# Talking-heads attention and a feed-forward layer on one core: second head mixing on 64x64 tiles, a new ordering pass, one ring of accumulator banks

## Chip, cores and metric

One core of one Trainium2 chip runs the whole program. The metric is the device time of one execution in microseconds (us); the kernel before takes 929.02 us as the median of three runs (928.87 to 931.21). Engines are called as in the profile: PE (matrix multiply) with its weight loads PEld, DVE (vector), ACT (scalar), POOL (GpSimd) and SP (which issues the DMAs).

## What is computed

Four batches, 12 heads, 448 positions, 64 elements per head, model width 768, feed-forward width 2048:

```python
scores = scale * np.matmul(q, k.transpose(0, 1, 3, 2))
scores = np.einsum('bhij,hg->bgij', scores, w_pre)      # first mixing of the heads
attn = softmax(scores, axis=-1)
attn = np.einsum('bhij,hg->bgij', attn, w_post)         # second mixing
x = np.matmul(attn, v)                                  # heads side by side: 1792 x 768
h = x @ w_in
out = (h * sigmoid(1.702 * h)) @ w_out
```

The feed-forward weights arrive as 64-bit floats, everything else as 32-bit floats.

## The kernel before

**Attention.** The unit of work is a step: 10 query rows of one batch, so 45 steps per batch and 180 in all. Score products (`scores`, tile `qk`) are made for blocks of about 112 rows, written to DRAM (`sd`) and read back (`gather`, tile `r`, four buffers) with one partition per row and head. `mix_two` (L321) mixes the heads of two steps in four 64x64 products (tile `mx`), `peak` takes row maxima on DVE, `expo` the exponential and row sums on ACT (tile `e`), `shifted`, `inverse` and `weigh_mix` divide the mixing matrix by the sums (tile `wr`). `post` (L368) is the second mixing. It turns the attention around at the same time, so that positions j come to lie on partitions: the exponentials are the stationary operand in four slices of CP = 112 columns, for two halves of the rows (a = 0, 1), and `wr` is the moving operand with 60 columns. That is 8 products of 32-bit floats for one step, into one pair of accumulator banks (tile `pp`, one buffer):

```python
for jc in range(NR):
    for a in range(2):
        rs = slice(a * GAP, a * GAP + w)
        nc.tensor.matmul(pp[:CP, a, jc*w:(jc+1)*w], e[rs, jc*CP:(jc+1)*CP], wr[rs, :, :n], ...)
```

The pair is then copied out by ACT (`keep_whole`, first two batches) or split into two 16-bit parts by ACT and DVE (`keep_upper`, `keep_lower`). `context` (tile `av`) multiplies by V.

**Feed-forward.** 32 units (8 slices of the width for each of 4 batches). A unit has 36 products in `hidden` (L578, tile `h`) and 36 in `project` (L622, tile `po`), in 16-bit floats with two parts per operand. The weights of a slice are converted once (`conversion`, L484: ACT, POOL and DVE make two 16-bit parts in the tile `w_p`, tag `wc`, one buffer), stored to DRAM (`wd`, `store`) and loaded again for each of the four batches (`fetch_w`, L574, tile `wt`: 64 loads of 768 KB).

**What sets the order.** Nothing is ordered by the hardware or a library: `add` (L676) notes each job with its engine, an assumed duration, a due time and the buffers that it takes; `run_all` (L740) goes through the jobs once, always taking one that can start soonest and is due first, and writes the instructions in that order. Where it foresees an idle stretch of PE it has `fill` (L287) put in products of a matrix of ones whose result is not used (L290). Accumulator banks come from a pool: six single banks in turn (`gen`) and the one pair (`pp`).

Of the kernel before, what the change touches and what calls it, by code (L numbers as in the profile page):

```python
# [1 line left out]

# [34 lines left out]
NR, CP = 4, S // 4  # L37
NCC = DM // 128
NS = 8
# [6 lines left out]
def attention_then_feed_forward(ctx, tc, q, k, v, w_pre, w_post, w_in, w_out, out):  # L46
# [16 lines left out]
    NBK = 6  # L63
# [54 lines left out]
    def add_over(parts):  # L118

        p, n = parts.shape  # L120
        t = bank(f"sums_{len(first_sum)}")[:, :n]
        first_sum.append(n)
        nc.tensor.matmul(t, ones[:p, :], parts, start=True, stop=True)
        return t
# [6 lines left out]
    SH = {"q": [128, NPAIR // THIRDS, S], "k": [128, NPAIR // THIRDS, S], "v": [CP, H // THIRDS, NR * D]}  # L131
# [55 lines left out]
    def pair_of(name, b, i):  # L187

        key = (name + "p", b, i)
        if key not in st:  # L190
            if name == "v":
                st[key] = flow.tile([CP, 2, H // THIRDS, NR * D], F16, name=f"vp{i}_{b}", tag=f"vp{i}")
# [33 lines left out]
    def bank(name, tag="gen", bufs=NBK):  # L226
        return ps.tile([128, 512], F32, name=name, tag=tag, bufs=bufs)

    def scores(b, c, pr, tag=("gen", NBK)):

        i0, n = block(b, c)
        two = [bank(f"qk_{b}_{c}_{pr}_{x}", *tag) for x in range(2)]
# [82 lines left out]
    def mix(i):  # L315
        mx = row["mx", i] = bank(f"mx_{i}")
        fill(mx)
        r = row.pop(("r", i))
        nc.tensor.matmul(mx[:, :S], wa, r[:KG], start=True, stop=True)  # L319

    def mix_two(two):  # L321

        tiles = []
        for y, i in enumerate(two):
            mx = row["mx", i] = bank(f"mx_{i}")
# [42 lines left out]
    def post(i):  # L368
# [26 lines left out]
    def keep_whole(i):  # L395
        nc.scalar.copy(mixed_to(i), row.pop(("pp", i)))  # L396
# [10 lines left out]
    def context(b, c, pr):  # L407
        i0, n = chunk(b, c)
        if pr % 3 == 0:
            av = bank(f"av_{b}_{c}_{pr}")  # L410
# [4 lines left out]
        if not AV16[b]:  # L415
            for jc in range(NR):
                for d in range(2):
# [3 lines left out]
                        st["v", b, h // w][:, h % w, jc * D:(jc + 1) * D],  # L421
# [5 lines left out]
        for t, (jc, i, j) in enumerate(terms):  # L427
            for d in range(2):
# [3 lines left out]
                    st["vp", b, h // w][:, i, h % w, jc * D:(jc + 1) * D],  # L432
# [47 lines left out]
    NP = 3  # L480
    HW = WN // NP
    WF = 5

    def conversion(kind, s):  # L484

        nm = f"w{kind}_{s}"
        src = (w_in, w_out)[kind][s]
# [83 lines left out]
    wt = {}  # L571
# [6 lines left out]
    def hidden(u, fc, part):  # L578

        s, b = units[u]  # L580
        if part == 0:
            st["h", u, fc] = bank(f"h_{u}_{fc}")[:, :S]
            fill(st["h", u, fc])
# [38 lines left out]
    def project(u, e):  # L622
        g, w = gt[u], wt[1, u].rearrange("p t (f e) -> p t f e", e=DM)
        po = st["po", u, e] = bank(f"po_{u}_{e}")[:, :S]
# [37 lines left out]
    COUNT = {"r": NRB, "e": 3, "wr": NWR, "pp": 1, "gen": NBK, "sc": 3, "p": 2, "x": 2,  # L662
# [4 lines left out]
    waiting, lanes = [], []  # L667
# [6 lines left out]
    MODE = {"qk": 1, "pp": 1, "mx": 2, "av": 3}  # L674

    def add(eng, occ, f, after=(), due=0.0, lat=None, size=0.0, takes=(), kind="", bias=0.0, behind=None, moves=""):  # L676

        occ = occ if isinstance(occ, dict) else {e: occ for e in eng.split("/")}
        if lat is None:
# [3 lines left out]
             "kind": kind, "moves": moves, "bias": bias, "left": 0, "then": [], "next": [], "at": None, "from": 0.0}  # L683
# [9 lines left out]
        if not j["left"]:  # L693
            waiting.append(j)
# [10 lines left out]
    def room_for(j, e):  # L705

        at, need = 0.0, {}
        for x in j["takes"]:
            if len(x) == 2 or x[2] == e:
# [8 lines left out]

    def take(j, e):
        for x in j["takes"]:  # L720
            if len(x) == 2 or x[2] == e:
                have = held[x[0]]
                if len(have) >= COUNT[x[0]]:
                    done = [(over_when(h), n) for n, h in enumerate(have) if over_when(h) is not None]
                    have.pop(min(done)[1])
# [14 lines left out]
    def run_all():  # L740

        last = ""
        while waiting:
            picks = []
            for e in list(free) + ["-"]:
# [15 lines left out]
                if best:  # L761
                    t = min(x[0] for x in best) + LOOK
                    picks.append(min((x for x in best if x[0] <= t), key=lambda x: (x[2]["due"] - (2.0 if e == "PE" and last in MODE and x[2]["kind"] in MODE else 0.0), x[0]))[1:] + (e,))
            assert picks, [(j["eng"], j["due"], [x[0] for x in j["takes"]]) for j in waiting][:20]
            s, j, e = min(picks, key=lambda x: (x[0], x[1]["due"]))
            waiting.remove(j)
# [18 lines left out]
            log.append((s, e, j))  # L785
            j["by"] = e
            settle(j, at, e, 0.0 if j["size"] else CROSS)
            j["f"](e) if len(j["eng"]) > 1 else j["f"]()
            gap[0] = 0.0

    log = []
# [44 lines left out]
    idle = ps.tile([128, 512], F32, name="idle", tag="gen", bufs=NBK)  # L836
# [67 lines left out]
    tags = [("gen", NBK)]*3  # L904
    near = st["near"] = mixed.tile([CI, H, S], F32, name="near", tag="p")
    for pr in range(NPAIR):
        two = scores(0, 0, pr, tags[pr % 3])
# [14 lines left out]
    held["gen"] = [12.0, 12.2, 12.6, 12.9, 13.2, 13.5]  # L922
# [18 lines left out]
    def step_tasks(i):  # L941
# [4 lines left out]
        if i < GPC:  # L946
# [3 lines left out]
            if i < AHEAD:  # L950
                m["from"] = READY[i]
        else:
            if g % 2 == 0:
                two = [i, i + 1] if g + 1 < GPB else [i]
                for x in two:
                    mx_home[x] = []
                m = add("PE", 0.77, lambda: mix_two(two), [gathers[x] for x in two] + [mixes.get(i - 1), mixers.get(b)], i - 1,
                        takes=[("gen", mx_home[x]) for x in two], kind="mx")
# [14 lines left out]
        p = add("PE", 0.44, lambda: post(i), [w, e, posts.get(i - 1)], i + 1, takes=[("pp", pp)], kind="pp")  # L973
# [104 lines left out]
    def conversion_tasks(kind, s, first):  # L1078
# [17 lines left out]
        for a in range(NP):  # L1096
            u = add("A", 0.62, lambda a=a: c["w_upper"](a, "A"), [k] + low[:0] + ([ups[0]] if a else []), due + 0.5, 0.72,
                    takes=[] if a else [("wc", pair)])
# [6 lines left out]
        pair.append(j)  # L1105


    at_scores = {}
# [65 lines left out]
    for u in range(NU + 1):  # L1174
        for fc in range(2):
# [4 lines left out]
            if u:  # L1180
                quanta += [("p", u - 1, e) for e in range(3 * fc, 3 * fc + 3)]
    due_of = {q: BEGIN + n / RATE for n, q in enumerate(quanta)}
    g_done, rests = {}, {}
    wt_home = {(kind, u): [] for kind in range(2) for u in range(NU)}
    got = {}
    for u in range(NU):
        s, b = units[u]
        due = due_of["h", u, 0, 0]
        for kind in range(2):
            got[kind, u] = add("SP", 0.4, lambda kind=kind, u=u: fetch_w(kind, u),  # L1190
                               [conv_done[kind, s]] + gated_by(min(int(due) - 14, N)), due - 6 + 3 * kind,
                               size=0.786, takes=[(f"wt{kind}", wt_home[kind, u])], kind="late", behind=got.get((kind, u - 1)), moves="wt")
        g_home, lower_g = [], []
        for fc in range(SF):
            gen, th = [], []
            j = None
            for x in range(3):
                due = due_of["h", u, fc, x] - 1.5 * (x > 0)
                j = add("PE", 1.134, lambda u=u, fc=fc, x=x: hidden(u, fc, x), [got[0, u], x_done[b], j], due,
                        takes=[] if x else [("gen", gen)], kind="ff")  # L1200
# [15 lines left out]
        for e in range(NCC):  # L1216
            due = due_of["p", u, e]
            gen, pt = [], []
            j = add("PE", 1.134, lambda u=u, e=e: project(u, e), [got[1, u], *lower_g], due, takes=[("gen", gen)], kind="ff")
            g_home.append(j)  # L1220
            wt_home[1, u].append(j)
# [5 lines left out]
            def both(by, u=u, e=e, s=s, b=b, k=(k := {})):  # L1227
                collect(u, e, by)
                if by == "D" or s == 0:
                    k["rest"]["eng"], k["rest"]["occ"], k["rest"]["lat"] = ("-",), {"-": 0.0}, {"-": 0.0}  # L1230
# [3 lines left out]
                     {x: rest[x] + 0.1 for x in eng.split("/")}, takes=takes, bias=0.8)  # L1234

# [16 lines left out]
def _layout(inputs):  # L1252
# [4 lines left out]
    a["v"] = a["v"].reshape(B, H, NR, CP, D).transpose(0, 3, 1, 2, 4).reshape(B, CP, H, NR * D)  # L1257
# [26 lines left out]
```

## Time and profile before

| | us |
|---|---|
| median of three runs | 929.02 |
| profiled execution, its own time | 927.6 |
| span of its instructions | 925.9 |
| PE busy | 901.5 |
| ACT busy | 562.6 |
| DVE busy | 542.5 |

A timeline row gives the start, the time from the first start to the last end, the engine, the line of the kernel, the operation, the tile written and those read, sizes and count. Products are pipelined, so that a row reaches into the next one: what a group costs is the distance from its start to the start of the next group. A product of 32-bit floats is two weight loads and two matmul records.

### The profile page before, as it was taken

The page shows a single profiled execution, that of the slowest core. Times are in us where ns is not written, and L with a number is a line of the kernel's source. Part 1 is how long each engine was busy: PE and PEld are TensorE (multiplying, and loading weights), DVE is VectorE, ACT ScalarE, POOL GpSimd, SP SyncE. Part 2 cuts the span into 40 slices and gives each one's busy share as a digit, 9 for nine tenths or more (in the row PEclk, how much of TensorE's full clock was granted, in tenths as well). Part 3 has the DMA queues.
Part 4 walks back from the last instruction along what each step waited for, and adds up shares of the span by engine and source line. Part 5 has one row for each costly group of instructions (what it writes and reads, how often), then busy time and mean ns, then how long its engine had stood idle before and what let it go on. Part 6 is the DMA issues. An engine that isn't in the chain of part 4 may idle for free.

```text
span 925.9 us, 22628 instructions
## 1 busy us (share of the span) xinstructions
PE 901.5 (97%) x8708; PEld 548.3 (59%) x8708; DVE 542.5 (59%) x1254; ACT 562.6 (61%) x1280; POOL 264.6 (29%) x518
## 2 busy tenths in 40 slices
PE   8998998999999999989999999999999999999998
PEld 4676676556565665655656555555656555555554
DVE  4656665876768977975456755457544553333233
ACT  4867776887678697854576565555555453323442
POOL 1312332332223513351116322332123332203332
PEclk9999999999999999999999999999999999999999
DMA  6878888889878998776677585466544322344322
GB/s 218 279 234 264 268 292 267 301 297 286 301 250 284 293 319 273 254 242 212 208 249 225 159 263 164 142 206 214 174 142 125 126 95 69 123 142 137 137 70 93
DMA packets 68270, 194.42 MB, mean 210 GB/s; under 512 B 10419, under 2 KB 35123, under 8 KB 68163
## 3 DMA queue, kind: packets, MB, share of 16 engines
q1 hardware_dynamic: 68163, 192.98, 63.9%
q8 instruction: 69, 1.13, 0.5%
q14 instruction: 38, 0.31, 0.1%
HBM read 136.32 MB, written 54.04 MB: 206 GB/s over the span
## 4 chain that ended last, share of the span: by engine, by line
PE 89%; DVE 5%; ACT 2%; DMA 2%; issue 1%; POOL 0%; SPq 0%; ACTq 0%; DVEq 0%; POOLq 0%
PE h L589 23%; PE po L628 23%; PE pp L377 16%; PE mx L333 7%; PE av L419 4%; PE qk L239 3%; PE av L430 3%; PE pp L290 3%; PE qk L249 3%; PE mx L319 1%; DMA qf<-in_q_dram 1%; ACT p L396 1%; DVE w_f L518 1%; DVE nm L338 1%; DVE w_p L557 1%
## 5 line engine op out<-in xcount | busy, mean ns | idle before, releaser
L589 PE MATMUL h<-x,wt 128*128 128x448 f16 x1152 | 244.2, 353 | 0.0
L628 PE MATMUL po<-g,wt 128*128 128x448 f16 x1152 | 241.4, 353 | 0.1
L377 PEld LDWEIGHTS pp<-wr,e 60*112 60x112 f32 (+1 forms) x2880 | 158.3, 175 | 62.9 <-issue 40.0
L377 PE MATMUL pp<-wr,e 60*112 60x60 f32 (+1 forms) x2880 | 177.8, 262 | 0.0
L628 PEld LDWEIGHTS <-wt 128*128 128x128 f16 x1152 | 108.9, 98 | 113.6 <-issue 17.9
L589 PEld LDWEIGHTS <-wt 128*128 128x128 f16 x1152 | 108.4, 98 | 103.5 <-issue 6.6
L656 POOL TENSOR_TENSOR acc<-acc,pt 128x448 f32<-128x448 f32 x83 | 99.6, 1201 | 149.6 <-ACT pt L650 141.4
L355 POOL TENSOR_SCALAR rs<-sm 124x1 f32<-124x1 f32 x180 | 44.5, 247 | 328.0 <-ACT e L345 325.4
L345 ACT ACTIVATE e<-mx,nm 124x448 f32<-124x448 f32 x180 | 114.6, 637 | 20.9 <-DVE nm L338 20.0
L338 DVE TENSOR_REDUCE nm<-mx 124x1 f32<-124x448 f32 x180 | 107.7, 616 | 26.8 <-PE mx L333 20.0
L608 DVE SCALAR_TENSOR_TENSOR th<-th,h 128x448 f32<-128x448 f32 x64 | 39.6, 619 | 137.1 <-ACT th L604 136.9
L650 ACT ACTIVATE pt<-po,ct 128x448 f32<-128x448 f32 x83 | 52.4, 633 | 84.4 <-PE po L628 81.6
L404 DVE TENSOR_TENSOR p<-pp,p 112x480 f16<-112x480 f32 (+1 forms) x90 | 58.7, 652 | 70.9 <-ACT p L400 70.8
L400 ACT CAST p<-pp 112x480 f16<-112x480 f32 (+1 forms) x90 | 50.5, 562 | 72.0 <-PE pp L377 71.5
L333 PE MATMUL mx<-r,wq 60*64 60x448 f32 (+1 forms) x672 | 84.5, 562 | 0.0
L396 ACT COPY p<-pp 112x480 f32<-112x480 f32 (+1 forms) x90 | 51.1, 567 | 40.1 <-PE pp L377 39.3
L604 ACT ACTIVATE th<-h,ct 128x448 f32<-128x448 f32 x64 | 40.5, 633 | 55.5 <-PE h L589 55.2
L652 DVE SCALAR_TENSOR_TENSOR acc<-po,ct,acc 128x448 f32<-128x448 f32 x85 | 57.6, 680 | 23.4 <-PE po L628 23.2
L260 ACT COPY sc<-qk 112x448 f32<-112x448 f32 (+1 forms) x124 | 61.8, 539 | 13.9 <-PE qk L249 9.2
L614 ACT ACTIVATE g<-th,gs 128x448 f16<-128x448 f32 x64 | 42.8, 668 | 24.3 <-DVE th L608 23.8
L508 POOL TENSOR_SCALAR w_f<-w_f 128x512 f32<-128x512 f32 x48 | 32.1, 670 | 74.3 <-ACT w_f L504 73.3
L366 POOL TENSOR_SCALAR wr<-wp,rs 124x60 f32<-124x60 f32 (+1 forms) x90 | 38.9, 433 | 48.6 <-DVE rs L360 34.7
(137 smaller groups left out, 1018.3 us busy)
## 6 DMA issues: line engine op xcount, KB each, us to landing
wt<-wd SPq DMA_DIRECT2D x64, 768.0 KB
r<-sd SPq DMA_DIRECT2D x317, 105.0 KB
sd<-sc SPq DMA_DIRECT2D x84, 392.0 KB
w<-in_moe_w_in_dram SPq DMA_DIRECT2D x24, 512.0 KB
w<-in_moe_w_out_dram SPq DMA_DIRECT2D x24, 512.0 KB
wd<-w_p SPq DMA_DIRECT2D x16, 768.0 KB
out_dram<-acc SPq DMA_DIRECT2D x24, 224.0 KB
kf<-in_k_dram SPq DMA_DIRECT2D x6, 448.0 KB
```

Of the source, the lines that this page charges most:

```text
L260: (nc.scalar.copy if eng == "A" else nc.vector.tensor_copy)(t[:n, x, :], two[x][:n, :S])
L333: nc.tensor.matmul(out, w[rs], r[rs], start=True, stop=True)
L338: nc.vector.tensor_reduce(nm[:K], row["mx", i][:K, :S], axis=AX.X, op=ALU.max, negate=True)
L345: nc.scalar.activation(e[:K], row.pop(("mx", i))[:K, :S], AF.Exp, bias=row.pop(("nm", i))[:K, 0:1], accum_out=sm[:K, 0:1],)
L377: nc.tensor.matmul(pp[:CP, a, jc * w:(jc + 1) * w], e[rs, jc * CP:(jc + 1) * CP], wr[rs, :, :n], start=True, stop=True,)
L396: nc.scalar.copy(mixed_to(i), row.pop(("pp", i)))
L404: nc.vector.tensor_tensor(p[1], row.pop(("pp", i)), p[0], op=ALU.subtract)
L589: nc.tensor.matmul(h, w[:, i, c, fc * 128:(fc + 1) * 128], x[:, j, c, :], start=(n == 0), stop=(n == len(terms) - 1),)
L628: nc.tensor.matmul(po, w[:, j, fc, e * 128:(e + 1) * 128], g[:, i, fc, :], start=(n == 0), stop=(n == len(terms) - 1),)
L650: nc.scalar.activation(pt, po, AF.Copy, scale=c)
L652: nc.vector.scalar_tensor_tensor(a, po, c, a, op0=ALU.mult, op1=ALU.add)
L656: nc.gpsimd.tensor_tensor(a, a, st.pop(("pt", u, e)), op=ALU.add)
```

## The change

1. `post` works on 64x64 tiles: each slice of 112 positions is cut in two of CJ = 56, which go to the lower and the upper 64 partitions. The lower one loads 64 columns (8 of them over again, against zero rows that `_layout` puts into V). A step has 16 products in the place of 8. The kept tiles have CP = 120 partitions, V tiles 128.
2. The eight banks form one tile, `banks`. The ordering pass gives out bank numbers; a step takes any two neighbours.
3. `run_all` goes through the jobs up to 15 times without writing: after each forward pass, `latest` goes backward from the end and finds how late each job could start; these times rank the jobs in the next pass. The best pass is written. The assumed duration of `post` is the same as before.
4. Converted weights are written straight into the `wt` buffers that the first batch reads (`DIRECT = 0`), besides the store to DRAM; the first batch's 16 loads fall away.
5. Loads of the 64-bit weights may start 20 steps earlier, `mix_two` is queued behind an earlier `post`, and `keep_whole` may run on ACT or DVE.

Cut to its core:

```diff
-NR, CP = 4, S // 4
+NR, CJ = 4, S // 8
+CP = 64 + CJ
...
-        pp = ps.tile([128, 2, 512], F32, name=f"pp_{i}", tag="pp", bufs=1)
+        pp = bank(2)
         fill(pp[:, 0])
         for jc in range(NR):
-            for a in range(2):
-                rs = slice(a * GAP, a * GAP + w)
-                nc.tensor.matmul(
-                    pp[:CP, a, jc * w:(jc + 1) * w], e[rs, jc * CP:(jc + 1) * CP], wr[rs, :, :n],
-                    start=True, stop=True,
-                )
+            for d in range(2):
+                j0, m = (2 * jc + d) * CJ, CJ if d else GAP
+                for a in range(2):
+                    rs = slice(a * GAP, a * GAP + w)
+                    nc.tensor.matmul(
+                        pp[d * GAP:d * GAP + m, a, jc * w:(jc + 1) * w], e[rs, j0:j0 + m], wr[rs, :, :n],
+                        start=True, stop=True,
+                    )
...
+        to = dict(tag=f"wt{kind}", bufs=2) if s >= DIRECT else dict(tag="wc", bufs=1)
...
-                t["p"] = flow.tile([128, 2, WN], F16, name=f"{nm}_p", tag="wc", bufs=1)
+                t["p"] = flow.tile([128, 2, WN], F16, name=f"{nm}_p", **to)
+                if s >= DIRECT:
+                    wt[kind, s] = t["p"]
...
-    MODE = {"qk": 1, "pp": 1, "mx": 2, "av": 3}
+    MODE = {"qk": 1, "pp": 2, "mx": 2, "av": 3}
...
+        for n in range(PASSES + 1):
+            reset(ranks)
+            order = one_pass(False)
+            if order is None:
+                break
+            end = max(j["at"] for j in jobs)
+            if best is None or end < best[0]:
+                best = end, ranks, STAY[0]
+            ENDS.append(end)
+            ranks = latest(order)
+            STAY[0] = STAYS
+        reset(best[1])
+        STAY[0] = best[2]
+        one_pass(True)
...
-            q = add("A", 0.47, lambda: keep_whole(i), [p], i + 2, 0.58, takes=takes_p)
+            q = add("A/D", {"A": 0.47, "D": 0.53}, lambda e: keep_whole(i, e), [p], i + 2, {"A": 0.58, "D": 0.62}, takes=takes_p, bias=0.3)
...
-            j = add("SP", 0.4, lambda a=a: c["fetch"](a), gated_by(first + 2 * a), first + 2 * a, size=0.524, takes=[("w64", w64)], kind="late", moves="w64")
+            j = add("SP", 0.4, lambda a=a: c["fetch"](a), gated_by(first + 2 * a - 20), first + 2 * a, size=0.524, takes=[("w64", w64)], kind="late", moves="w64")
```

How the order moves, counted over the whole program: products of ones fall from 176 to 94; the places where PE goes from one tile shape (128x128, 64x128, 128x64, 64x64) to another fall from 463 to 346; the copies of L396 that go to DVE are 17 of 90; `collect` goes to ACT and POOL 70 times in the place of 83, to DVE 98 in the place of 85; loads `wt<-wd` fall from 64 to 48. The first feed-forward product stands behind the 47th `post` before, behind the 45th now.

PE, before, around the end of the first chunk of 12 steps (`r`: gathered scores, `p`: kept attention, `vf`: V):

```order
L333 MATMUL mx_750<-r_663,wq 64x448 x2
L333 MATMUL mx_751<-r_668,wq 64x448 x2
L419 MATMUL av_0_3_770<-p_0_311,vf_0_547 64x120 x8
L419 MATMUL av_0_3_770<-p_0_311,vf_0_632 64x120 x16
L377 MATMUL pp_834<-wr_824,e_767 112x60 x8
L290 MATMUL pp_864<-ones 128x128 x4
L377 MATMUL pp_864<-wr_831,e_808 112x60 x8
```

and the same place now:

```order
L345 MATMUL banks<-r_628,wq 64x448 x2
L345 MATMUL banks<-r_660,wq 64x448 x2
L391 MATMUL banks<-wr_774,e_762 64x60 x2
L391 MATMUL banks<-wr_774,e_762 56x60 x2
L391 MATMUL banks<-wr_774,e_762 64x60 x2
L391 MATMUL banks<-wr_774,e_762 56x60 x2
L391 MATMUL banks<-wr_774,e_762 64x60 x2
L391 MATMUL banks<-wr_774,e_762 56x60 x2
L391 MATMUL banks<-wr_774,e_762 64x60 x2
L391 MATMUL banks<-wr_774,e_762 56x60 x2
```

A second mixing of eight products over 112 positions is now sixteen over 64 and 56; it stands right behind a first mixing, with the same tile shape, and the context product that stood between them has moved.

SP, before, where the first batch's weights are loaded for the first time (`w`: 64-bit weights, `sd`: scores):

```order
L497 DMA w_2_64_0_2023<-in_moe_w_out_dram 128x1024
L264 DMA sd_0_97<-sc_0_4_2011 112x896
L576 DMA wt_0_2064<-wd_0_109 128x3072
L264 DMA sd_0_97<-sc_0_5_2057 112x896
L264 DMA sd_1_98<-sc_1_2_2075 112x896
```

and now:

```order
L583 DMA wd_0_118<-w_0_p 128x3072
L515 DMA w_2_64_0_2223<-in_moe_w_out_dram 128x1024
L276 DMA sd_1_98<-sc_1_2_2189 112x896
L276 DMA sd_1_98<-sc_1_3_2200 112x896
L276 DMA sd_0_97<-sc_0_4_2226 112x896
L515 DMA w_2_64_1_2307<-in_moe_w_out_dram 128x1024
```

The store of converted weights remains, later than before; the load of them for the first batch is gone.

## Rows read from the trace of the kernel before

**Rows 1.** The page: span, then busy time of each engine, share, instructions.

```profile
span 925.9 us, 22628 instructions
PE 901.5 (97%) x8708; PEld 548.3 (59%) x8708; DVE 542.5 (59%) x1254; ACT 562.6 (61%) x1280; POOL 264.6 (29%) x518
```

**Rows 2.** The page: the chain that ended last, by engine and by line.

```profile
PE 89%; DVE 5%; ACT 2%; DMA 2%; issue 1%; POOL 0%; SPq 0%; ACTq 0%; DVEq 0%; POOLq 0%
PE h L589 23%; PE po L628 23%; PE pp L377 16%; PE mx L333 7%; PE av L419 4%; PE qk L239 3%; PE av L430 3%; PE pp L290 3%; PE qk L249 3%; PE mx L319 1%; DMA qf<-in_q_dram 1%; ACT p L396 1%; DVE w_f L518 1%; DVE nm L338 1%; DVE w_p L557 1%
```

**Rows 3.** Busy time by stretch, all engines: length, PE, PEld, DVE, ACT, POOL, clock, DMA share, GB/s.

```profile
0.00:20.00 20.00, 17.31 (x72) 9.69 (x72) 8.82 (x25) 8.68 (x18) 1.80 (x15) 1.00 0.60 208
20.00:160.00 140.00, 131.25 (x1506) 95.57 (x1506) 84.95 (x215) 102.19 (x252) 40.74 (x105) 0.99 0.85 271
160.00:420.00 260.00, 251.25 (x2447) 156.19 (x2444) 204.46 (x489) 196.23 (x469) 87.42 (x166) 0.99 0.85 280
420.00:785.00 365.00, 364.61 (x3842) 214.91 (x3841) 199.71 (x434) 206.03 (x464) 96.21 (x198) 1.00 0.55 174
785.00:926.00 141.00, 137.12 (x853) 71.99 (x851) 44.55 (x91) 49.51 (x81) 38.46 (x34) 1.00 0.33 115
```

**Rows 4.** The same stretches, products of ones (L290) alone: PE, PEld.

```profile
20.00:160.00 140.00, 29.40 (x198) 24.94 (x198) 0.99 0.85 271
160.00:420.00 260.00, 21.71 (x148) 19.29 (x148) 0.99 0.85 280
420.00:785.00 365.00, 1.20 (x6) 0.82 (x6) 1.00 0.55 174
```

**Rows 5.** Timeline of PE, 511.9 to 516.4 us.

```profile
510.78 1.30 PE L628 MATMUL po<-g,wt 128*128 128x448 f16 x6
511.92 1.30 PE L589 MATMUL h<-x,wt 128*128 128x448 f16 x6
513.15 1.00 PE L377 MATMUL pp<-wr,e 60*112 60x60 f32 x16
514.07 0.98 PE L333 MATMUL mx<-r,wq 60*64 60x448 f32 x8
514.99 1.31 PE L628 MATMUL po<-g,wt 128*128 128x448 f16 x6
```

**Rows 6.** Timeline of PE, 66 to 69 us: a post between products of its own tile shape.

```profile
66.97 0.91 PE L377 MATMUL pp<-wr,e 60*112 60x60 f32 x16
67.71 0.96 PE L239 MATMUL qk<-kf,qf 64*104 64x448 f32 x4
```

**Rows 7.** Timeline of PEld in 5 ns windows at 513.32 and 513.42 us.

```profile
513.24 0.18 PEld L377 LDWEIGHTS pp<-wr,e 60*112 60x112 f32 x2
...
513.34 0.18 PEld L377 LDWEIGHTS pp<-wr,e 60*112 60x112 f32 x2
```

**Rows 8.** Timeline of PEld at 514.07 and 514.23 us, and of PE at 514.48 us.

```profile
514.07 0.15 PEld L333 LDWEIGHTS mx<-r,wq 60*64 60x64 f32 x4
...
514.13 0.15 PEld L333 LDWEIGHTS mx<-r,wq 60*64 60x64 f32 x4
...
514.07 0.61 PE L333 MATMUL mx<-r,wq 60*64 60x448 f32 x4
```

**Rows 9.** Timeline of PE, two context products and what follows each.

```profile
503.18 2.08 PE L430 MATMUL av<-p,vp 112*64 112x120 f16 x72
505.20 1.12 PE L628 MATMUL po<-g,wt 128*128 128x448 f16 x5
...
593.89 1.60 PE L430 MATMUL av<-p,vp 112*64 112x88 f16 x72
595.42 0.80 PE L377 MATMUL pp<-wr,e 60*112 60x60 f32 x12
```

**Rows 10.** Groups by form on PE: busy us, mean ns, idle before, what ended it.

```profile
L290 PE MATMUL pp<-ones 128*128 128x128 f32 x204 | 28.8, 292 | 12.9 <-ACT p L396 9.4 <-DVE p L404 2.1 <-DVE rs L360 1.5
```

**Rows 11.** Second mixing (L377) alone in the third and fourth stretch: PE, PEld.

```profile
160.00:420.00 260.00, 55.10 (x896) 49.10 (x896) 0.99 0.85 280
420.00:785.00 365.00, 78.18 (x1264) 68.84 (x1264) 1.00 0.55 174
```

**Rows 12.** The page, groups of POOL, DVE and ACT that move (columns as in rows 10).

```profile
L656 POOL TENSOR_TENSOR acc<-acc,pt 128x448 f32<-128x448 f32 x83 | 99.6, 1201 | 149.6 <-ACT pt L650 141.4
...
L650 ACT ACTIVATE pt<-po,ct 128x448 f32<-128x448 f32 x83 | 52.4, 633 | 84.4 <-PE po L628 81.6
L404 DVE TENSOR_TENSOR p<-pp,p 112x480 f16<-112x480 f32 (+1 forms) x90 | 58.7, 652 | 70.9 <-ACT p L400 70.8
...
L396 ACT COPY p<-pp 112x480 f32<-112x480 f32 (+1 forms) x90 | 51.1, 567 | 40.1 <-PE pp L377 39.3
...
L652 DVE SCALAR_TENSOR_TENSOR acc<-po,ct,acc 128x448 f32<-128x448 f32 x85 | 57.6, 680 | 23.4 <-PE po L628 23.2
```

More of the change, by code (lines that the diff above doesn't have):

```diff
@@ L315, in mix @@
     def mix(i):
-        mx = row["mx", i] = bank(f"mx_{i}")
+        mx = row["mx", i] = bank()
         fill(mx)
@@ L707, in room_for @@
         at, need = 0.0, {}
+        at = min((x[0] for x in places(j)), default=None) if any(x[0] in BANKS for x in j["takes"]) else 0.0
+        if at is None:
+            return None
         for x in j["takes"]:
+            if x[0] in BANKS:
+                continue
             if len(x) == 2 or x[2] == e:
@@ L762, in run_all @@
                     t = min(x[0] for x in best) + LOOK
[L763 to L766, printed above, removed]
+                    picks.append(min((x for x in best if x[0] <= t), key=lambda x: (x[2]["rank"] - (STAY[0] if e == "PE" and last in MODE and x[2]["kind"] in MODE else 0.0), x[0]))[1:] + (e,))
+            if not picks:
+                return None
+            s, j, e = min(picks, key=lambda x: (x[0], x[1]["rank"]))
+            del waiting[next(n for n, x in enumerate(waiting) if x is j)]
             take(j, e)
@@ new lines, in latest, with last_place, put @@
+    def latest(order):
+        end = max(j["at"] for j in jobs)
+        over = {}
+        used = {e: ([], []) for e in [*free, "ring", "port"]}
+        def last_place(use, ub, width):
+            starts, ends = use
+            x = bisect.bisect_left(starts, ub + width) - 1
+            t = ub
+            while x >= 0 and ends[x] > t:
+                t = min(t, starts[x] - width)
+                x -= 1
+            return t
+        def put(use, s, t):
+            starts, ends = use
+            x = bisect.bisect_left(starts, s)
+            if x < len(starts) and starts[x] <= t + 1e-9:
+                t = max(t, ends[x])
+                del starts[x], ends[x]
+            if x and ends[x - 1] >= s - 1e-9:
+                ends[x - 1] = max(t, ends[x - 1])
+            else:
+                starts.insert(x, s)
+                ends.insert(x, t)
+        left = {id(j): len(j["then"]) + len(j["next"]) + len(j["frees"]) for j in jobs}
+        before = {id(j): [] for j in jobs}
+        for j in jobs:
+            for x in j["then"] + j["next"] + j["frees"]:
+                before[id(x)].append(j)
+        ready = [(-j["at"], n) for n, j in enumerate(jobs) if not left[id(j)]]
+        number = {id(j): n for n, j in enumerate(jobs)}
+        heapq.heapify(ready)
+        while ready:
+            j = jobs[heapq.heappop(ready)[1]]
+            e = j["by"]
+            gap = 0.0 if j["size"] else CROSS
+            by = [end]
+            for x in j["then"]:
+                by.append(over[id(x)] - (0.0 if e == "-" else SAME if x["by"] == e else gap))
+            by += [over[id(x)] - CROSS for x in j["frees"]]
+            by = min(by)
+            if j["size"]:
+                width = j["size"] / 16 / DMA["rate"]
+                t = last_place(used["ring"], by - DMA["late"] - MARGIN.get(j["moves"], 0.0) - width, width)
+                put(used["ring"], t, t + width)
+                t -= DMA["issue"]
+            else:
+                t = by - j["lat"][e]
+            t = min([t] + [over[id(x)] - 0.01 for x in j["next"]])
+            if e != "-":
+                width = j["occ"][e]
+                uses = [used[e]] + [used["port"]] * (j["kind"] == "two" and e in "DG")
+                old = None
+                while old != t:
+                    old = t
+                    for u in uses:
+                        t = last_place(u, t, width)
+                for u in uses:
+                    put(u, t, t + width)
+            over[id(j)] = t
+            for x in before[id(j)]:
+                left[id(x)] -= 1
+                if not left[id(x)]:
+                    heapq.heappush(ready, (-x["at"], number[id(x)]))
+        assert len(over) == len(jobs)
+        low = min(over.values())
+        return [over[id(j)] - low for j in jobs]
@@ L957, in step_tasks @@
                 m = add("PE", 0.77, lambda: mix_two(two), [gathers[x] for x in two] + [mixes.get(i - 1), mixers.get(b)], i - 1,
-                        takes=[("gen", mx_home[x]) for x in two], kind="mx")
+                        takes=[("gen", mx_home[x]) for x in two], kind="mx", behind=posts.get(i - 3))
                 for x in two:
@@ L972, in step_tasks @@
         w = add("G", 0.35, lambda: weigh_mix(i), [v], i, 0.3, takes=[("wr", wr)])
-        p = add("PE", 0.44, lambda: post(i), [w, e, posts.get(i - 1)], i + 1, takes=[("pp", pp)], kind="pp")
+        p = add("PE", 0.44, lambda: post(i), [w, e, posts.get(i - 1)], i + 1, takes=[("two", pp)], kind="pp")
         wr.append(p)
@@ L1105, in conversion_tasks @@
         pair.append(j)
+        if s >= DIRECT:
+            wt_home[kind, s] = pair
+            got[kind, s] = low
+            wt_taken[kind, s] = ups[0]
+    wt_home = {(kind, u): [] for kind in range(2) for u in range(B * NS)}
+    got, wt_taken = {}, {}
     at_scores = {}
```

159 lines of the change are left out of this document (115 added, 44 removed).

## Prediction, made blind

> **What bounds the kernel now.** I read the page first: PE is busy 97% of the span, ACT 61%, DVE 59% [rows 1], and the chain that ended last lies on PE for 89% [rows 2]. A busy PE alone proves little, since products overlap and some are made only to fill. So next the stretches. From 420 us on PE is never idle: 364.6 of 365 us busy, while DVE and ACT work 200 and 206 us [rows 3]; whatever PE is spared there comes off the end, as long as the other engines keep up. Before that PE is idle for 8.75 us in 20-160 and 8.75 us in 160-420 (length less busy time), and 29.4 and 21.7 us more go to products of ones [rows 3, 4]. Idle time and fillers together are 17.9 + 52.3 = 70 us in which PE stood and something else was late. The last 141 us are feed-forward alone, and the granted clock is 0.99 to 1.00 throughout, so it is no term. So nearly all of the time is PE's own work, and the question is what that work costs when it is cut differently.
>
> The costly item is the second mixing, 16% of the chain [rows 2]. The timeline shows one post starting at 513.15 and its successor at 514.07: 0.92 us [rows 5]. Of this a part is the change of tile shape: six feed-forward products take 1.14 us when their own kind follows and 1.23 us when a post follows [rows 5], so a change costs 0.09 us. A post between products of its own shape takes 0.74 us [rows 6]. Inside it the weight loads set the pace: two of 112 columns, one for each half of the rows, start every 0.10 us [rows 7], eight times (16 records). Its 60 moving columns hide under that.
>
> **The change part by part.**
>
> *Second mixing.* Now a post has 16 products, 32 pairs of weight load and matmul record, spread over four tiles: eight rounds of four. The first mixing already shows such a round: four loads of 64 columns start together at 514.07, the next four at 514.13, and four matmuls run side by side [rows 8]. That is 0.06 us for a round. By columns it would be 0.74 / 8 x 64 / 112 = 0.053 us. I take 0.057, between them, as the row's two decimals leave that open: 8 x 0.057 = 0.46 us. The saving is 0.28 us for each of 180 posts: 51 us (47 at 0.06, 57 at 0.053). On the path are all 180 as far as PE is the last to be ready: 45 of them lie before 160 us, 56 in the second stretch, 79 after 420 (x896 and x1264, 16 to a post) [rows 11].
>
> Here the skill speaks against the change. The Trainium skill, page "TensorEngine Tiling (Array Packing)", section Instruction Overhead, puts about 60 cycles on each matmul and advises against taking a tiling factor from a dimension that is already small; 60 moving columns are small. By that, as an estimate from the page, 32 pairs at 25 ns are 0.80 us, and the second mixing would gain nothing. The trace so far contradicts it where several tiles are in use: 72 pairs in 593.89 to 595.42 are 21 ns each, over two tiles only [rows 9], and the four matmuls above need no such spacing [rows 8]. What no row shows is 32 pairs in a row over four tiles; this is the first rival and the third.
>
> *Changes of shape.* The order has 117 fewer (463 to 346), since first and second mixing now share a shape and the order groups them: 117 x 0.09 = 10.5 us, all on PE. Where PE waits anyway it is worth nothing; most of the places lie in the stretch without waits, so I keep it.
>
> *Waits and fillers (70 us now).* The single pair of `pp` banks made PE wait 9.4 us for ACT's copy and 2.1 us for DVE's before fillers [rows 10]; with any two of eight banks these 11.5 us can go. The order has 82 fewer products of ones; at 52.3 us for 176 they cost 0.30 us each, so 24 us, if nothing else is late in their place. Against it: PE arrives earlier at each wait, by about 0.3 us in a step, so that part of the wait that is now hidden behind a slow post comes out. Bounds: nothing is gained (PE waits 70 us as before), or only the 94 products are left (28 us, a gain of 42). I take 20, the bank waits and a third of the fillers, and not more, because 160-420 has DVE at 79% and DMA at 85% [rows 3].
>
> *Weights written in place.* 16 loads of 768 KB go: 12.6 MB, about 45 us of the DMA's rate of 280 GB/s, in a stretch where DMA is 85% busy [rows 3]. No wait of PE on these loads is in the chain [rows 2], so the sum takes nothing for it; it is the room that lets the other transfers keep up. The price is a new wait: from the third unit on, ACT's first `w_upper` needs the buffer of the unit two before it, and in ACT's queue exponentials stand behind it, on which PE's posts depend. Between lies a unit of 72 products, 72 x 0.19 = 13.7 us by [rows 5] (1.14 us for six), so I price it at nothing; without that cover each of twelve such places could cost the microseconds of one conversion.
>
> *Moved work.* 17 copies go from ACT to DVE (0.65 us each by the nearest DVE row, 0.57 on ACT), 13 collections from ACT and POOL to DVE (0.68 us; 0.63 and 1.20 saved) [rows 12]: DVE gets 20 us more, ACT 18 less, POOL 16 less. Hidden after 420 us (DVE 55% busy); in 160-420 it uses up part of the room. V tiles grow by a seventh and the copies from 112 to 120 partitions with the same 480 elements: nothing.
>
> **Sum.** Against the profiled execution: 927.6 - 51 - 10.5 - 20 = 846. The median of the runs shown is 1.4 us above that execution (929.0), so I predict **847 us**. With the ends of the three terms this likeliest case runs from 929 - 57 - 10.5 - 42 = 819 to 929 - 47 - 10.5 - 0 = 872.
>
> **Rivals.**
>
> *1. The pairs do not follow each other that fast.* If 32 pairs need the 21 ns of the context run [rows 9], a post takes 0.68 us, the saving is 0.06 x 180 = 11 us in the place of 51, and the time is 887. For it: nothing in the trace is denser over so many pairs. Against: that run is itself filled by its moving columns (88 over two tiles), so 21 ns is an upper bound, and rows 8. Chance 0.10.
>
> *2. The early stages are held by something else.* If DVE, DMA and the step's own chain (mixing, maximum, exponential, sum, product) keep 20-420 at its length, only 79 posts and their share of the changes count: 22 + 5 = 27 us, time 902. For it: DMA 85% busy, DVE 204 of 260 us [rows 3]. Against: PE's own work, fillers left out, is still 73% and 88% of the two stretches, ACT and DVE in 20-160 are at 73% and 61%, and a sixth of the DMA bytes of the second stretch leave. Chance 0.11.
>
> *3. Slower: the pairs run one after another whatever their tile.* The place is L391. At the 28 ns of the 120-column context run (2.02 us for 72 [rows 9]) a post takes 32 x 0.028 = 0.90 us, 0.16 more, 28 us in all; less 10.5 for the changes of shape and with the waits as they are, 947. It decides from 25 ns on: there a post takes 0.80 us and the changes of shape are just used up. For it: twice as many instructions through one queue. Against: rows 8. Chance 0.03 for this, and 0.03 for ending within the bound of no change, around that point. By the skill's page above it would be this point exactly.
>
> **How the numbers follow.** 0.73 for the forecast, 0.10 and 0.11 for the first two rivals, 0.03 and 0.03 for the rest. A measurement of this kernel tells about 0.3%, 3 us, from no change. Faster: 0.73 + 0.10 + 0.11 = 0.94; same 0.03; slower 0.03. The range is 818 to 885: the likeliest case with its ends, and most of the first rival; the second stays out.
>
> **What would show it.** Right: eight rounds of four weight loads in a post, one every 0.053 to 0.06 us; a post between feed-forward products taking about 0.65 us in the place of 0.92; PE above 97% after some 380 us, the all-feed-forward end as long as before (about 140 us); `pp` waits on copies gone. Wrong: rounds of 0.085 us or more (rival 1), PE idle or filling for 100 us or more in the first half (rival 2), a post over 0.9 us (rival 3).

## The result and the profile after

The changed kernel takes 851.61 us (median of four runs, 850.99 to 851.93) against 928.94 us for the kernel before in the same comparison: a ratio of 0.9163, 95% interval 0.9146 to 0.9181. The prediction was 847, range 818 to 885. The profiled execution has a span of 849.2 us where the one before had 925.9. The ratios here and below take executions in the fast state only; of the four in the first set with the old second mixing that leaves two, 899.76 and 912.78 us.

The page of the changed kernel: busy time, share and instructions of each engine, then the chain that ended last, by engine and by line.

```profile
PE 817.7 (96%) x11424; PEld 475.8 (56%) x11424; DVE 561.7 (66%) x1281; ACT 548.5 (65%) x1255; POOL 259.1 (31%) x503
...
PE 75%; DVE 8%; ACT 7%; DMA 6%; issue 3%; POOL 1%; SPq 0%; ACTq 0%; DVEq 0%; POOLq 0%
PE banks L608 23%; PE banks L647 22%; PE banks L391 9%; PE banks L345 6%; PE banks L251 3%; PE banks L444 3%; PE banks L433 3%; PE banks L261 2%; PE banks L302 2%; DMA r<-sd 2%; ACT e L357 1%; ACT waste L114 1%; DMA sd<-sc 1%; ACT sc L272 1%; DVE w_p L577 1%
```

PE works 84 us less, with more instructions. The second mixing (now L391) has gone from 16% of the chain to 9% [rows 2], and the chain leaves PE more often: 25% of it lies elsewhere, 11% before.

The stretches of the changed kernel, cut so that each holds as many posts as in [rows 3]: 45, 56 and 79. The other work in them is not quite the same: 24 feed-forward products already lie in the first one. All engines:

```profile
20.00:145.00 125.00, 112.73 (x2212) 77.95 (x2209) 92.21 (x238) 96.92 (x246) 45.27 (x107) 0.99 0.89 295
145.00:378.00 233.00, 223.78 (x3202) 127.34 (x3200) 202.94 (x472) 193.21 (x459) 91.97 (x161) 0.98 0.81 266
378.00:708.00 330.00, 326.24 (x5073) 187.29 (x5072) 211.30 (x455) 198.00 (x449) 81.73 (x187) 0.99 0.60 194
708.00:850.00 142.00, 137.49 (x856) 72.30 (x854) 44.62 (x91) 49.75 (x81) 38.55 (x35) 1.00 0.33 114
```

The second mixing alone, PE and PEld (x1440, x1792 and x2528 are 45, 56 and 79 posts of 32 records, as many as before):

```profile
20.00:145.00 125.00, 29.96 (x1440) 25.43 (x1440) 0.99 0.89 295
145.00:378.00 233.00, 38.67 (x1792) 31.83 (x1792) 0.98 0.81 266
378.00:708.00 330.00, 53.80 (x2528) 47.05 (x2528) 0.99 0.60 194
```

The products of ones alone:

```profile
20.00:145.00 125.00, 19.77 (x124) 16.79 (x124) 0.99 0.89 295
145.00:378.00 233.00, 9.53 (x64) 8.66 (x64) 0.98 0.81 266
378.00:708.00 330.00, 0.00 (x0) 0.00 (x0) 0.99 0.60 194
```

The three stretches were 140, 260 and 365 us [rows 3]; now they are 125, 233 and 330: 15, 27 and 35 us shorter. The feed-forward end is as long as before. Fillers have gone from 52.3 to 29.3 us [rows 4], but PE's idle time in the three stretches has risen from 17.9 to 25.2 us (length less busy time). Measured from post to post, the 45th ends at 132 us (157 before), the 101st at 377 (417), the last at 704 (781).

The timeline of PE in the changed kernel, two posts between feed-forward products and before a first mixing:

```profile
395.36 0.68 PE L391 MATMUL banks<-wr,e 60*64 60x60 f32 x32
395.98 2.44 PE L647 MATMUL banks<-g,w_p 128*128 128x448 f16 x12
398.35 0.68 PE L391 MATMUL banks<-wr,e 60*64 60x60 f32 x32
398.83 0.96 PE L345 MATMUL banks<-r,wq 60*64 60x448 f32 x8
```

Before a feed-forward product a post costs 0.62 us, before a first mixing 0.48 us. Both were about 0.92 us before: [rows 5] has a post in front of a first mixing, and this is one between feed-forward products:

```profile
508.71 1.00 PE L377 MATMUL pp<-wr,e 60*112 60x60 f32 x16
509.64 1.31 PE L589 MATMUL h<-x,wt 128*128 128x448 f16 x6
```

32 pairs of load and matmul in 0.48 us are 15 ns each, closer together than any pair in the context run [rows 9]. The weight loads of a post of the changed kernel, from the timeline of PEld at 410.52 and 410.70 us:

```profile
410.50 0.14 PEld L391 LDWEIGHTS banks<-wr,e 60*64 60x64 f32 x4 [0.37 <-issue]
...
410.61 0.20 PEld L391 LDWEIGHTS banks<-wr,e 60*64 60x64 f32 x8
```

Four loads start together at 410.50 us, as in the first mixing [rows 8], and the third round of four starts at 410.61, so that a round takes about 0.055 us.

To see what each kind of work costs on PE, the time from each record's start to the next one's, less idle time, was added up over the whole trace, for this kernel and for those of the experiments below. Each column is one profiled execution, which can lie up to 5 us from the median of its kernel.

```
us                              before   after   64x64 post   old post   one pass   parted ring   reload   no fillers
second mixing                    163.5   101.9        103.7      164.2      105.5         103.1    103.1        106.1
first mixing                      89.6    84.8         87.8       90.8       84.9          91.1     85.2         90.0
feed-forward                     446.5   447.2        446.7      447.9      447.9         450.0    446.5        447.1
scores and context               141.7   144.9        146.0      140.7      146.5         144.9    143.0        147.5
fillers and idle                  68.3    54.5         85.8       46.0       68.0          61.3     70.0         40.1
last record of a post at         781.0   703.5        741.6      759.8      723.5         725.3    718.8        701.6
```

(64x64 post: the kernel before with this part alone. Old post: the changed kernel without it, second measurement. The last row is a time from the start, not a sum.)

### The profile page after: what moved, and what is told of

The parts are those of the page before. It is cut to its first block, busy times and chain, and to the rows that moved or that the text cites. A ratio compares the mean times of both kernels' runs of the same rounds, so it can differ in the third digit from the quotient of the medians.

```text
span 849.2 us, 28127 instructions
## 1 busy us (share of the span) xinstructions
PE 817.7 (96%) x11424; PEld 475.8 (56%) x11424; DVE 561.7 (66%) x1281; ACT 548.5 (65%) x1255; POOL 259.1 (31%) x503
## 4 chain that ended last, share of the span: by engine, by line
PE 75%; DVE 8%; ACT 7%; DMA 6%; issue 3%; POOL 1%; SPq 0%; ACTq 0%; DVEq 0%; POOLq 0%
PE banks L608 23%; PE banks L647 22%; PE banks L391 9%; PE banks L345 6%; PE banks L251 3%; PE banks L444 3%; PE banks L433 3%; PE banks L261 2%; PE banks L302 2%; DMA r<-sd 2%; ACT e L357 1%; ACT waste L114 1%; DMA sd<-sc 1%; ACT sc L272 1%; DVE w_p L577 1%
## 5 line engine op out<-in xcount | busy, mean ns | idle before, releaser
L608 PE MATMUL banks<-x,wt 128*128 128x448 f16 x864 | 185.3, 354 | 0.0
L647 PE MATMUL banks<-g,wt 128*128 128x448 f16 x864 | 181.4, 353 | 2.0 <-issue 2.0
L391 PEld LDWEIGHTS banks<-wr,e 60*64 60x64 f32 (+2 forms) x5760 | 104.3, 131 | 70.8 <-issue 36.3
L357 ACT ACTIVATE e<-banks,nm 124x448 f32<-124x448 f32 x180 | 114.5, 638 | 25.5 <-DVE nm L350 12.6
L391 PE MATMUL banks<-wr,e 60*64 60x60 f32 (+2 forms) x5760 | 122.4, 221 | 7.9 <-POOL wr L378 4.6
L350 DVE TENSOR_REDUCE nm<-banks 124x1 f32<-124x448 f32 x180 | 106.6, 615 | 18.7 <-PE banks L345 14.3
L345 PE MATMUL banks<-r,wq 60*64 60x448 f32 (+1 forms) x672 | 86.2, 545 | 0.7 <-DMA r<-sd 0.7
L272 ACT COPY sc<-banks 112x448 f32<-112x448 f32 (+1 forms) x128 | 65.0, 542 | 21.9 <-PE banks L261 13.0
L671 DVE SCALAR_TENSOR_TENSOR acc<-banks,ct,acc 128x448 f32<-128x448 f32 x98 | 66.2, 678 | 19.4 <-PE banks L647 18.5
L647 PE MATMUL banks<-g,w_p 128*128 128x448 f16 x288 | 61.4, 359 | 1.0 <-DVE g L637 1.0
```

The source lines that it names most:

```text
L272: (nc.scalar.copy if eng == "A" else nc.vector.tensor_copy)(t[:n, x, :], two[x][:n, :S])
L350: nc.vector.tensor_reduce(nm[:K], row["mx", i][:K, :S], axis=AX.X, op=ALU.max, negate=True)
L357: nc.scalar.activation(e[:K], row.pop(("mx", i))[:K, :S], AF.Exp, bias=row.pop(("nm", i))[:K, 0:1], accum_out=sm[:K, 0:1],)
L391: nc.tensor.matmul(pp[d * GAP:d * GAP + m, a, jc * w:(jc + 1) * w], e[rs, j0:j0 + m], wr[rs, :, :n], start=True, stop=True,)
L608: nc.tensor.matmul(h, w[:, i, c, fc * 128:(fc + 1) * 128], x[:, j, c, :], start=(n == 0), stop=(n == len(terms) - 1),)
L647: nc.tensor.matmul(po, w[:, j, fc, e * 128:(e + 1) * 128], g[:, i, fc, :], start=(n == 0), stop=(n == len(terms) - 1),)
```

## Experiments

Theory A: PE's own work bounds the kernel, so the cut of the second mixing carries most of the gain. Theory B: the new order and the ring carry it, and the shorter posts are hidden. Theory C: the first half is bound by DMA, and the weights written in place carry it.

**The changed kernel with the old second mixing** (order, ring and direct weights kept; V rows laid out to fit):

```diff
-            for d in range(2):
-                j0, m = (2 * jc + d) * CJ, CJ if d else GAP
-                for a in range(2):
...
+            for a in range(2):
+                rs = slice(a * GAP, a * GAP + w)
+                nc.tensor.matmul(
+                    pp[:CP, a, jc * w:(jc + 1) * w], e[rs, jc * CP:(jc + 1) * CP], wr[rs, :, :n],
...
```

> The changed kernel with its order, ring and direct weights, but the second mixing in 8 products over 112 columns as before (order of all instructions kept, V rows laid out to fit). Theory A (the cut into 64x64 tiles carries most of the gain, because PE's own work bounds the kernel): a post between feed-forward products goes from 0.61 back to 0.93 us, 0.32 x 180 = 57 us, and some 110 places between first and second mixing become changes of shape again, 0.09 each, 10 us; less what vanishes in the 54 us of waits and fillers: 902 to 917 us. Theory B (the new order and the ring carry it, the shorter posts are hidden): within 15 us of the changed kernel, 851 to 867.

Measured: 913.33 us (899.76 to 913.93), ratio 0.973 (0.963 to 0.983). In its profile PE's clock was at half for 31 us in one piece, so there is a second set of runs:

> The changed kernel with the second mixing of before, once more: its profile had one stretch of 31 us at half clock (27.7 to 58.4 us) and three of its four times at 913 us, one at 900. If the half clock belongs to this order with slow posts: most times at 910 to 915 again. If it was of that chip or run: most times at 897 to 903, and no stretch of more than 7 us at half clock.

Measured: 902.96 us (897.47 to 907.25), ratio 0.9702 (0.9662 to 0.9742). Stretches of the first of the two profiles, columns as above:

```profile
24.30:27.70 3.40, 1.57 (x18) 0.85 (x17) 2.28 (x6) 2.71 (x7) 2.47 (x5) 1.00 0.94 367
27.70:58.40 30.70, 30.37 (x155) 20.03 (x154) 10.53 (x31) 12.34 (x33) 6.59 (x19) 0.50 0.48 159
```

and of the second:

```profile
28.50:32.00 3.50, 3.50 (x26) 3.27 (x25) 2.15 (x5) 1.60 (x5) 2.17 (x5) 0.51 0.97 305
32.00:58.00 26.00, 26.00 (x303) 19.04 (x302) 14.14 (x37) 19.30 (x48) 7.73 (x23) 1.00 0.74 247
```

The 31 us at half clock do not come from the order alone: the second time the clock came back after 3.5 us. They were not one stray execution either, since three of the first four times are at 913 to 914 us with a mean clock of 0.97 to 0.98 and only one is at 900 with 0.99; the second set, on another chip, has 0.98 to 0.99. Two of the second set's four times lie above the 897 to 903 expected, and its longest piece at half clock is 10 us where 7 were expected at most, so neither expectation came out whole. Either way the old post takes the median back to 903 to 913, inside theory A's 902 to 917 (the lower one at its edge), far from B's 867. By the ratios the cut carries 5.4 to 5.7% of the time before, and everything else, with slow posts, 3%; PE then waits only 46 us. With the old posts this order has 408 changes of shape by the trace, 62 more than with the new ones, not the 110 of the expectation.

**The kernel before with the new second mixing alone** (order, pools and reloaded weights kept):

```diff
-            for a in range(2):
-                rs = slice(a * GAP, a * GAP + w)
...
+            for d in range(2):
+                j0, m = (2 * jc + d) * CJ, CJ if d else GAP
+                for a in range(2):
+                    rs = slice(a * GAP, a * GAP + w)
...
```

> The kernel before, its order, pools and reloaded weights kept, with the second mixing alone on 64x64 tiles. Theory A: PE is the bound after 420 us in the order before, so there 79 posts x 0.28 to 0.32 = 22 to 25 us come off for certain, and of the 101 earlier posts' 28 to 32 us about half: 875 to 893 us. If the order's waits were all due to PE, down to 872. Theory B: above 915 us.

Measured: 884.20 us against 931.65, ratio 0.9487 (0.9441 to 0.9532), inside theory A's 875 to 893. Its stretches, cut at the 45th, the 101st and the last post:

```profile
20.00:157.00 137.00, 122.42 (x2261) 84.98 (x2261) 85.47 (x216) 101.55 (x253) 40.17 (x104) 0.96 0.87 278
157.00:408.00 251.00, 236.56 (x3310) 139.60 (x3304) 202.16 (x489) 194.43 (x466) 85.41 (x166) 0.98 0.87 293
408.00:745.00 337.00, 335.23 (x5099) 187.98 (x5099) 198.01 (x434) 205.12 (x462) 95.67 (x198) 1.00 0.58 189
```

and its group of products of ones before posts, columns as in [rows 10]:

```profile
L291 PE MATMUL pp<-ones 128*128 128x128 f32 x204 | 33.1, 320 | 16.6 <-ACT p L399 11.3 <-DVE p L407 3.8 <-DVE rs L361 1.5
```

Where PE never waited, the third stretch, the whole saving arrives: 365 to 337 us, 28 us for 79 posts. In the first two, 101 posts are cheaper by some 32 us as well, but the stretches shrink by 3 and 9 only. PE arrives earlier and waits: fillers and idle rise from 68 to 86 us, and the wait for the single `pp` pair is longer (11.3 us for ACT's copies, 9.4 before). The profiled execution, 888.33 us, is the slowest of the four (882.32 to 888.33) and has some 20 us at half clock where the kernel before has 7, so the rise of 17 us is an upper value.

**One forward pass** in the place of up to 15: `PASSES = 0` for `PASSES = 14`.

> The changed kernel with its ordering in one forward pass (no backward passes); ring, direct weights and 64x64 posts kept. The order then has 411 changes of shape (346 with passes) and 145 products of ones (94). Theory A: 65 x 0.09 = 6 us for the shapes, 51 x 0.3 = 15 us for the fillers if they are real waits: 858 to 875 us. Theory B (the passes carry most of the gain): above 890.

Measured: 870.72 us, inside theory A's 858 to 875; ratio 0.934 (0.9302 to 0.9379): 1.8% of the time before above the changed kernel, 16 us. (The distances of this and the next runs from the changed kernel are differences of the ratios, since each set was compared with runs of the kernel before on its own chip.) The two profiled executions lie 20 us apart; 13.5 us of that are fillers and idle, 68.0 for 54.5, and 4 the second mixing, 105.5 for 101.9. The edit takes away more than the backward passes: a single pass also keeps the ordering's bias for staying in one tile shape at its first value (`STAY` 2.0, with passes `STAYS` 10.0). The two were not parted.

**The ring parted again:**

```diff
-            return [(max(free_at[x:x + 2]), x) for x in range(NBK - 1) if None not in free_at[x:x + 2]]
-        able = sorted((t, x) for x, t in enumerate(free_at) if t is not None)
+            return [(max(free_at[x:x + 2]), x) for x in (NBK - 2,) if None not in free_at[x:x + 2]]
+        able = sorted((t, x) for x, t in enumerate(free_at[:NBK - 2]) if t is not None)
```

> The changed kernel with the ring parted again: second mixings only in banks 6 and 7, all else in banks 0 to 5 (passes kept, order found anew: 424 changes of shape, 96 products of ones). Theory A: one pair makes each post wait for the copies of the one before: 78 x 0.09 = 7 us for shapes and up to 11 us of waits as in the kernel before: 852 to 870 us. Theory B2 (the ring is what lets the posts run): above 880.

Measured: 866.58 us, inside theory A's 852 to 870; ratio 0.9304 (0.9257 to 0.935), 13 us above the changed kernel. Waits of PE in this kernel (in total, times, longest):

```profile
PE banks L302 <- ACT p L410: 8.5, 13, 1.1
```

The wait for ACT's copy of the one pair, 9.4 us in the kernel before [rows 10] and absent from the changed kernel's fillers, is back, though fillers and idle together rise by 7 us only (61.3 for 54.5). Of the rest, 6 us are in the first mixing (91.1 for 84.8) and 3 in the feed-forward (450.0 for 447.2): the order now changes shape 424 times for 346. The profiled executions lie 18 us apart.

**Weights loaded again:** `DIRECT = 7` for `DIRECT = 0`.

> The changed kernel, but only the last of the eight weight slices is written in place; seven go through the one buffer and the store as before, so 14 of the 16 loads of 768 KB return (order found anew: 354 changes of shape, 150 products of ones in the place of 94). Theory A (PE's own work carries the gain; weights in place only give the other transfers room): 56 more fillers at 0.3 us, up to 17 us, with the end of the program untouched: 855 to 870 us. Theory C (DMA bounds the first half, so 11 MB at 280 GB/s, 39 us, come back whole): 885 or more.

Measured: 870.48 us, ratio 0.9372 (0.9354 to 0.9389), 19 us above the changed kernel. That is just above theory A's 855 to 870; theory C's 885 is far. Fillers and idle are 70.0 us. To part bytes from order, as many bytes were put back with the order kept, as a second store behind each first one and not as loads:

```diff
             nc.sync.dma_start(out=wd[kind, s], in_=t["p"])
+            nc.sync.dma_start(out=wd2[kind, s], in_=t["p"])
```

> The changed kernel, its order kept, with each of the 16 converted weight slices stored a second time (768 KB each, 12.6 MB in all, the bytes that the direct weights save, put back in the first half). If the loss of the run with reloaded weights (19 us) comes from DMA bytes: 10 to 20 us slower than the changed kernel, 861 to 872. If it comes from the order that the ordering pass finds with loads to wait for: within 5 us, 847 to 857.

Measured: 857.04 us, ratio 0.9236 (0.9202 to 0.9271): 7 us above the changed kernel, at the edge of the second expectation and 4 us below the first. Fillers and idle are 59.1 us by the same count. So the bytes are worth about a third of the 19 us, as far as stores stand for loads at other times. The rest is put down to the order found when loads must be waited for; that was not shown by a run of its own, and which wait in it costs most was not settled.

**No products of ones** (same order):

```diff
-        if gap[0] >= 0.5:
+        if False:
```

> The changed kernel with the same order and no products of ones (94 gone, 28 us of PE in the first half). If they stand in real waits, nothing moves: 848 to 856 us. If they hold up posts that could have started, 5 to 20 us faster: 832 to 847. If without them the granted clock falls to half over longer stretches (17 us at half in the profile of the changed kernel), slower: 856 to 875, with more of the first 365 us at half clock.

Measured: 852.30 us, ratio 0.9173 (0.9145 to 0.9201): no difference, as expected if they stand in real waits. Its first two stretches, cut at 146 and 365 us:

```profile
20.00:146.00 126.00, 104.16 (x2091) 67.69 (x2088) 92.61 (x237) 96.19 (x244) 45.62 (x107) 0.92 0.89 293
146.00:365.00 219.00, 203.04 (x2937) 112.35 (x2936) 189.22 (x435) 183.14 (x437) 82.07 (x150) 0.96 0.80 265
```

28 us of fillers go, PE's idle time rises from 27 to 40 us, and the granted clock falls to a mean of 0.92 and 0.96 (0.99 and 0.98 in the changed kernel). PE's other work gets a little dearer (the table: second mixing 4 us, first mixing 5, scores and context 3) and the time in waits, 54.5 us with fillers and now 40, shorter by about as much. The fillers stand in real waits and keep the clock up, and with these waits neither is worth anything.

**Four assumed durations set to the trace's** (two of the four edits are shown), then more passes too, `PASSES = 40` for `PASSES = 14`:

```diff
-        k = add("D", 0.64, lambda: peak(i), [m], i - 1, 0.73)
+        k = add("D", 0.56, lambda: peak(i), [m], i - 1, 0.7)
...
-        p = add("PE", 0.44, lambda: post(i), [w, e, posts.get(i - 1)], i + 1, takes=[("two", pp)], kind="pp")
+        p = add("PE", 0.47, lambda: post(i), [w, e, posts.get(i - 1)], i + 1, takes=[("two", pp)], kind="pp")
...
```

> The changed kernel with four assumed durations set to what its trace shows (post 0.47 in the place of 0.44 us, maximum 0.56 for 0.64, POOL's weigh 0.40 for 0.35 and its clamp 0.95 for 0.80); order found anew, 345 changes of shape, 111 fillers. If the 54 us of waits and fillers in the first half come from wrong durations: 835 to 848 us. If they come from the chain of a step and from DMA: 848 to 858.

> As the one before, with up to 40 passes in the place of 14 (340 changes of shape, 96 fillers). If more passes find a better order on the chip too: 3 to 10 us below the run before; if the order is at the mercy of what the durations leave out: within 5 us of it, either way.

Measured: 849.16 us, ratio 0.9136 (0.9116 to 0.9157), and 848.56 us, ratio 0.9135 (0.9107 to 0.9163). Both are about 2.5 us below the changed kernel, but the intervals overlap with its 0.9146 to 0.9181, so a gain is not shown. Forty passes add nothing. Fillers and idle are 51 us in both, so these four durations are not what most of the remaining 54 us come from.

The fifth part of the change (earlier loads of the 64-bit weights, `mix_two` behind an earlier `post`, `keep_whole` on ACT or DVE) was not undone by itself; what it is worth is not shown.

## Why the prediction was right

*Second mixing and changes of shape.* Predicted 51 + 10.5 us. PE's own work without fillers and idle fell by 63 us (852.4 to 789.5 by the table's method, small groups included). With the new post alone it fell by 57 (to 795.4), so that 6 of the 63 came with the new order, in which 96 of the 117 changes of shape vanish by the trace (463 before, 442 with the post alone, 346 now). The second mixing by itself fell by 62 us, 0.34 for each post where 0.28 were priced; part of what was priced as changes of shape is in it. The step "most of the places lie in the stretch without waits" is not right: 202 of the 463 lie after 420 us. A post takes 0.48 us in front of a first mixing (0.46 predicted) and 0.62 between feed-forward products (about 0.65). A round of four loads takes about 0.055 us, inside the 0.053 to 0.06 that were named as the sign of being right. The experiment with the new post alone and the one without it put the cut at 5.1% and at 5.4 to 5.7% of the time, together with its share of the shapes.

*The rule that spoke against it.* By the estimate made from the Trainium skill, "TensorEngine Tiling (Array Packing)", section Instruction Overhead, with its about 60 cycles for each matmul, a post would take 0.80 us. The trace does not agree: 0.48 us for 32 pairs, 15 ns each. The advice against a tiling factor from a dimension that is already small did not bear on this cut, which divides the 112 stationary columns and leaves the 60 moving ones whole. What did hold is that weight loads of different tiles overlap, as the first mixing had shown [rows 8]; the first rival's 21 ns was an upper bound and no more. Whether the loads or the issue of 32 pairs set the pace of a post now was not tried.

*Waits and fillers.* Predicted 20 us less; by the same reading 70.2 became 29.3 + 25.2 = 54.5, so 16 us less. The size is near, but the working does not bear it. The waits for copies of the one pair, 11.5 us before, are under 1 us now, as predicted. But the bound "nothing is gained" was not the worst case: the shorter posts by themselves add up to 17 us of waits (68 to 86 with the new post alone), and the ring, the passes and the direct weights then take up to 31 us out, nearly three times those 11.5 us. And these need each other: undone one at a time they cost 13, 16 and 19 us, 48 in all. That the sum of these came near 20 is in part luck.

*Weights written in place.* The step "the sum takes nothing for it" was wrong. Undoing most of it costs 19 us, about 7 of them by the bytes alone. The words beside it, that it is the room that lets the other transfers keep up, are borne out for those 7 us at most, and then room has a price: PE arrives earlier, and the DMA share in the first stretch is 0.89 where it was 0.85.

*The second rival.* It would have left the first 400 us as they were. With the old order it comes close to true: 140 + 260 us became 137 + 251. In the changed kernel they became 125 + 233, because order, ring and weights changed with the post. The third stretch gave 35 us where 27 were predicted for posts and shapes: 28 come from the post alone, and by the order 54 feed-forward products fewer stand between the 101st post and the last (1014 for 1068), 10 us at 0.19.

*The slower rival* had its sign at 25 ns for a pair; 15 ns were measured.

*The clock.* "No term" left out some microseconds: the changed kernel's profile has 17 us at half clock, the kernel before 7. At half clock work takes about twice as long, so 10 us more cost up to 5 us as an estimate from these two profiles, about what the forecast of 847 missed. It is not shown that they do: the run without fillers has 37 us at half clock and the same time.

## What to carry to other kernels

When weight loads of a narrow product set its pace, cutting the stationary operand across column tiles can pay even if the moving operand is short: here it did with the four tiles used in turn (0.74 to 0.48 us), and no other order of the tiles was tried. Look for another place in the same kernel where four tiles already run, and read the pace there. Make the sum by stretches: a saving on the bounding engine arrives whole only where that engine never waits, and elsewhere it turns into waits until buffers, transfers and order follow. Changes that seem worth nothing against the old waits can be worth 1 to 2% each against the new ones.

## What was not expected of the hardware

In one execution PE's clock stayed at 1.2 GHz (granted 0.50) from 27.7 to 58.4 us although PE was busy 30.4 of these 30.7 us; it had been idle for 1.8 us shortly before. PE's timeline there:

```profile
26.86 1.04 PE L388 MATMUL banks<-wr,e 60*112 60x60 f32 x16 [1.83 <-ACT w_f L519]
27.83 2.50 PE L301 MATMUL banks<-ones 128*128 128x128 f32 x10
30.26 1.75 PE L388 MATMUL banks<-wr,e 60*112 60x60 f32 x16
```

The same program in another execution, with an idle time of 2.1 us at the same place, was back at 2.4 GHz after 3.5 us. At half clock a post of the old form takes about 1.7 us, and the median of that set is 10 us above the second's (7 us if each is taken against the kernel before on its own chip). The other profiles show falls of 3.4 to 13.7 us each; the changed kernel has 17 us of them in all, the kernel before 7. What decides whether the clock comes back was not tried.
